# Strided attention scores and values in four quadrants of the array, and one engine for both query copies

## The chip, the core and the metric

The kernel runs on one core of one Trainium2 chip. The metric is the time of one execution on the device in microseconds, as the median of several runs; smaller is better. The core has a matrix engine (TensorE, PE in the profile, with its weight loads as PEld), a vector engine (VectorE, DVE), an activation engine (ScalarE, ACT), GpSimd (POOL) and SyncE (SP), which here issues DMA loads. TensorE writes its results to PSUM, eight banks of 2 KB in each of 128 partitions; the other engines read them from there.

## What is computed

Attention over 8 batches, 8 heads, 576 positions and 64 columns a head, and behind it a mixture of 8 experts. Four heads attend to the last 32 positions (local), the other four to the earlier positions with the same residue modulo 32 (strided). In short, from the reference:

```python
rel = pos[:, None] - pos[None, :]
mask_local = (rel >= 0) & (rel < 32)
mask_strided = (rel >= 0) & (pos[None, :] % 32 == pos[:, None] % 32)
scores = np.where(mask, q @ k.T / sqrt(64), -1e9)
attn = exp(scores - max); attn = attn / (sum(attn) + 1e-9)
x = attn @ v                      # (8*576, 512) for the experts
e = argmax(x @ w_gate + modality_bias)
out = gate * (relu(x @ w1[e]) @ w2[e])
```

So a strided head falls apart into 32 problems (residues) of 18 x 18 positions each.

## The kernel before, in words

Attention runs over 32 units, 16 local and 16 strided in turn (lines 965 to 972). A local unit is one head of two batches, a strided unit two heads of one batch. A step of the main loop (lines 1032 to 1076) works on four units at once: the scores of unit n, the transposes of unit n-2 (turn), the masks of unit n+1 and the value products of unit n-3; it also issues loads for units n+3 and n-1. Two steps, one strided and one local, are called a pair here, and a pair has the number of its strided unit, 0 to 15. After each 8 units a batch pair is complete: its rows are transposed (xl, xs), the router's products run (lg) and small steps on VectorE follow. Behind attention come the slots of the experts (L921, L935), which are not touched.

TensorE's order is the order of the code (manual_schedule, line 1029), and a few steps are pinned. The other engines' order, and which PSUM bank a tile gets, are chosen by a scheduler before the program runs. On the chip each engine works through its own list in order, and an instruction that waits holds up what stands behind it.

A strided unit before: prep copies the queries of the two heads into a tile qz whose other blocks are zero, one head by VectorE, one by ScalarE (L408). masks writes the mask into the score tile ss by a product with the identity (L412). scores makes 32 products (L419), one a residue: 36 stationary columns (two heads of 18 queries, 128 partitions high because qz has zeros) and 18 moving columns. VectorE takes the maximum (L431) and the difference (L433), ScalarE the exponential (L434), VectorE the row sum (L436), plus 1e-9 (L437), the reciprocal (L438) and the product (L440, tile ens). turn transposes in four pieces (tile ts) and spreads them into a block diagonal tile eb: VectorE writes two of four blocks (L450), ScalarE the others (L454). values makes 32 records from 16 products (L464) of 72 stationary rows, and ScalarE copies them from ot to xc (L472).

A local unit before: prep copies the queries of two batches into qd, one by VectorE and one by ScalarE (L317). Scores (L334) are followed by maximum and difference on VectorE for a tile of 256 and one of 320 columns (L341, L342), by exponentials on ScalarE (L343, L344), by transposes, by copies into et (L356, L359), by the products with the values (L369, L375) and by VectorE's normalisation (L380, L381, L382, tile xt). xl is copied by L495, xs by L488.

A float32 product shows as two matmul records and two weight loads in the profile.

Of the kernel before, what the change touches and what calls it, by code (L numbers as in the profile page):

```python
# [54 lines left out]
C_T = C_P + 1  # L55
C_F = C_T + 4
# [12 lines left out]
M_TRI = M_S + 16 * 18  # L69
# [13 lines left out]

def _constants():
# [7 lines left out]
    for t in range(4):  # L92
        cf[18 * t:18 * t + 18, C_T + t] = 1
# [13 lines left out]
    causal = np.where(a[None, :] <= a[:, None], 0, BIG)  # L107
    for j in range(2):
        for h in range(2):
            r0 = 64 * j + 18 * h  # L110
            cb[r0:r0 + 18, M_S:M_S + 288] = np.tile(causal, (1, 16))
# [6 lines left out]
def _layout(q, k, v, moe_modality_id, moe_w_gate, moe_modality_bias, moe_w1, moe_w2):  # L118
# [29 lines left out]
    vs = v[:, 4:].reshape(B, 2, 2, 18, 4, 2, 4, D).transpose(0, 1, 6, 3, 4, 5, 2, 7)  # L148
    vs = np.ascontiguousarray(vs).reshape(B, 2, 72, 1024)
# [33 lines left out]
def attention_moe(ctx: ExitStack, tc: tile.TileContext, a, out):  # L183
# [103 lines left out]
    qzs = zeros(2, [P, 32, 2, 18], "qz")  # L287
    for t in qds + ets:
        nc.vector.memset(t[:], 0.0)
    for t in qzs:  # L290
        nc.gpsimd.memset(t[:], 0.0)


    class Local:
# [92 lines left out]
    class Strided:  # L387
# [10 lines left out]
        def load_values(self, part, last):  # L398
            if part == 0:
                self.vs = lp.tile([72, 8, 2, D], F32, tag="vs", name=f"vs{self.n}")  # L400
                behind(nc.sync.dma_start(self.vs.rearrange("p g h d -> p (g h d)"), a["vs"][self.b, self.pr]), last)

        def prep(self):
            self.qz = qz = qzs[self.n % 2]
            for h in range(2):
                r = slice(64 * h, 64 * h + 64)
                dst, src = qz[r, :, h, :], self.qk[r, 0, :].rearrange("p (r q) -> p r q", q=18)
                pin(nc.scalar.copy(dst, src) if h else nc.vector.tensor_copy(dst, src))  # L408

        def masks(self):  # L410
            self.s = pa(f"ss{self.n}")[:, :288]
            nc.tensor.matmul(self.s, identb, cb[:, M_S:M_S + 288], start=True, stop=True)  # L412

        def scores(self):
            n, qz, s = self.n, self.qz, self.s
            for i in range(16):
                for j in range(2):
                    r = (i // 4) * 8 + j * 4 + i % 4
                    at["scores"] = nc.tensor.matmul(  # L419
                        s[64 * j:64 * j + 36, 18 * i:18 * i + 18],  # L420
                        qz[:, r, :, :].rearrange("p h q -> p (h q)"),
                        self.qk[:, 1, 18 * r:18 * r + 18],
                        start=False, stop=True, skip_group_check=True,
                    )
            s3 = s.rearrange("p (i k) -> p i k", i=16)

            def bc(t):
                return t.unsqueeze(2).to_broadcast([P, 16, 18])

            mx = lp.tile([P, 16], F32, tag="mxs", name=f"mxs{n}")  # L430
            nc.vector.tensor_reduce(mx[:], s3, AX.X, ALU.max)  # L431
            ex = lp.tile([P, 16, 18], F32, tag="exs", name=f"exs{n}")
            nc.vector.tensor_tensor(ex[:], s3, bc(mx), ALU.subtract)  # L433
            nc.scalar.activation(ex[:], ex[:], AF.Exp, scale=0.125)  # L434
            sm = lp.tile([P, 16], F32, tag="sms", name=f"sms{n}")
# [3 lines left out]
            self.en = lp.tile([P, 16, 18], F32, tag="ens", name=f"ens{n}")  # L439
            nc.vector.tensor_tensor(self.en[:], ex[:], bc(sm), ALU.mult)  # L440

        def turn(self):
            n = self.n
            tp = pa(f"ts{n}").rearrange("p (g q) -> p g q", g=4)
            for g in range(4):
                turned_to(tp[0:72, g, :], self.en[:, 4 * g:4 * g + 4, :])
            self.eb = eb = lp.tile([72, 8, 4, 36], F32, tag="eb", name=f"eb{n}")
            src = tp[0:72].rearrange("p g (j x) -> p (g j) x", j=2)[:, :, 0:36]
            sh = [72, 8, 2, 36]
            nc.vector.tensor_tensor(  # L450
                eb[:, :, 0:2, :], src.unsqueeze(2).to_broadcast(sh),
                cf[0:72, C_T:C_T + 2].unsqueeze(1).unsqueeze(3).to_broadcast(sh), ALU.mult)
            for t in (2, 3):
                nc.scalar.activation(eb[:, :, t, :], src, AF.Copy, scale=cf[0:72, C_T + t:C_T + t + 1])  # L454

        def values(self):
            n, eb, vs, b = self.n, self.eb, self.vs, self.b
            for g2 in range(2):
                ot = pa(f"ot{n}{g2}")[:, :288]
                for g in (2 * g2, 2 * g2 + 1):  # L460
                    for j in range(2):
                        c = (g % 2) * 144 + 72 * j
                        for h in range(2):
                            at["values"] = nc.tensor.matmul(  # L464
                                ot[64 * h:64 * h + 64, c:c + 72],
                                vs[:, 2 * g + j, h, :],
                                eb[:, 2 * g + j, :, 18 * h:18 * h + 18],
                                start=True, stop=True, skip_group_check=True,
                            )
                base = (b % 2) * S  # L470
# [676 lines left out]
```

## Time and profile before

| | before |
|---|---|
| median of 3 runs | 598.16 us (596.69 to 599.0) |
| profiled execution | 600.58 us |
| its span, first to last instruction | 598.8 us |
| TensorE busy | 574.2 us (96%) |
| VectorE busy | 439.1 us (73%) |
| ScalarE busy | 395.0 us (66%) |
| GpSimd busy | 249.0 us (42%) |
| mean granted TensorE clock | 0.986 |

A busy share is a mean over the span. Attention fills the first 163 us or so, and there the engines stand otherwise than in the rest; the stretches below are taken from it. "Idle before" names what ended a wait, not what caused it.

### The profile page before, as it was taken

Reading aid. Unit: us, or ns where it says so; the run is one execution under the profiler, and the core shown is the slowest. Engines: PE = TensorE matmul, PEld = TensorE weight load, DVE = VectorE, ACT = ScalarE, POOL = GpSimd, SP = SyncE. Lnnn points to the kernel's source line nnn. Section 1 sums busy time; section 2 is a strip of 40 time slices with the busy share of each in tenths; the row PEclk is TensorE's granted clock in tenths of the full one; section 3 lists DMA queues with packets and bytes.
Section 4 is the critical chain, followed back from the end, with each engine's and each line's share of the span. In section 5 each row is a group of like instructions: output and inputs, shape, how many; then the busy total and the mean of one; then the engine's idle time right before and its main releaser. Section 6 shows DMA issues by size and latency. Waiting matters only on the chain.

```text
span 598.8 us, 15262 instructions
## 1 busy us (share of the span) xinstructions
PE 574.2 (96%) x5995; PEld 508.0 (85%) x5997; DVE 439.1 (73%) x1092; ACT 395.0 (66%) x814; POOL 249.0 (42%) x226
## 2 busy tenths in 40 slices
PE   8998889897999999999999999999999999999995
PEld 5887778776879898999999989999999999999995
DVE  6885967954868799668687687687687787787542
ACT  5897868764785676676566576665665665665652
POOL 1021101126247636554544746546545646532311
PEclk9999989988899999999999999999999999999998
DMA  8997978987745843744843844213214239514631
GB/s 316 301 295 218 346 242 282 318 293 248 253 108 159 235 146 97 235 156 103 243 153 98 221 168 92 71 37 106 71 36 106 71 113 278 110 45 71 221 103 50
DMA packets 72482, 102.03 MB, mean 170 GB/s; under 512 B 48019, under 2 KB 48275, under 8 KB 68820
## 3 DMA queue, kind: packets, MB, share of 16 engines
q0 software_dynamic: 20672, 58.01, 29.1%
q1 hardware_dynamic: 51252, 42.48, 26.7%
q8 instruction: 49, 0.80, 0.6%
q10 hardware_dynamic: 480, 0.51, 0.3%
q14 instruction: 29, 0.24, 0.1%
HBM read 123.45 MB, written 19.18 MB: 238 GB/s over the span
## 4 chain that ended last, share of the span: by engine, by line
PE 85%; DVE 4%; issue 4%; DMA 3%; ACT 2%; POOL 0%; SPq 0%; POOLq 0%; ACTq 0%; DVEq 0%
PE h L921 34%; PE o L935 33%; PE o L369 3%; PE ot L464 2%; DMA vs<-in_vs 2%; PE s L334 2%; PE ss L419 2%; PE xs L218 1%; PE lg L524 1%; PE t L218 1%; PE ts L218 1%; PE xl L218 1%; DMA qks<-in_qks 1%; PE en L620 1%; ACT wh L956 1%
## 5 line engine op out<-in xcount | busy, mean ns | idle before, releaser
L957 DVE TENSOR_TENSOR wl<-raw,wh 128x512 fp32r<-128x512 f32 x288 | 187.8, 692 | 66.0 <-ACT wh L956 52.5
L956 ACT CAST wh<-raw 128x512 fp32r<-128x512 f32 x288 | 163.9, 619 | 71.5 <-PE o L935 49.5
L921 PE MATMUL h<-xh,wl 128*128 128x256 f32 x576 | 162.7, 283 | 0.0
L921 PE MATMUL h<-xl,wh 128*128 128x256 f32 x576 | 162.6, 283 | 0.0
L921 PE MATMUL h<-xh,wh 128*128 128x256 f32 x576 | 162.4, 282 | 0.2 <-ACT wh L956 0.2
L803 POOL DMA_INDIRECT raw<-in_w,wi x72 | 92.6, 1286 | 158.1 <-DVE wl L957 121.4
L921 PEld LDWEIGHTS h<-xh,wh 128*128 128x128 f32 x576 | 109.5, 190 | 7.6 <-issue 0.6
L921 PEld LDWEIGHTS h<-xl,wh 128*128 128x128 f32 x576 | 109.6, 190 | 5.5
L935 PE MATMUL o<-wh,hh 128*128 128x512 f32 x288 | 114.3, 397 | 0.0
L935 PE MATMUL o<-wl,hh 128*128 128x512 f32 x288 | 113.8, 395 | 0.0
L921 PEld LDWEIGHTS h<-xh,wl 128*128 128x128 f32 x576 | 109.7, 190 | 1.0
L935 PE MATMUL o<-wh,hl 128*128 128x512 f32 x288 | 110.3, 390 | 0.0
L924 ACT ACTIVATE hh<-h 128x256 fp32r<-128x256 f32 x144 | 55.4, 384 | 67.2 <-PE h L921 50.1
L926 DVE SCALAR_TENSOR_TENSOR hl<-h,hh 128x256 fp32r<-128x256 f32 x144 | 60.7, 421 | 30.7 <-ACT hh L924 23.4
L935 PEld LDWEIGHTS o<-wh,hl 128*128 128x128 f32 x288 | 53.5, 188 | 11.0
L935 PEld LDWEIGHTS o<-wh,hh 128*128 128x128 f32 x288 | 54.6, 189 | 7.8 <-ACT hh L924 0.2
L935 PEld LDWEIGHTS o<-wl,hh 128*128 128x128 f32 x288 | 54.6, 190 | 5.6
L943 POOL DMA_INDIRECT out<-y,le x36 | 44.2, 1229 | 20.7 <-ACT y L942 11.0
L794 POOL DMA_INDIRECT le<-ld,li x36 | 39.6, 1101 | 12.9 <-issue 10.1
L787 POOL DMA_INDIRECT fx<-xd,le x36 | 40.1, 1115 | 11.0 <-issue 10.7
L479 POOL DMA_DIRECT2D xd<-xt x20 | 14.5, 725 | 61.9 <-ACT xt L488 61.9
L369 PEld LDWEIGHTS o<-vv,et 128*64 128x64 f32 x512 | 21.2, 156 | 10.1 <-issue 7.6
(192 smaller groups left out, 779.8 us busy)
## 6 DMA issues: line engine op xcount, KB each, us to landing
vv<-in_vl SPq DMA_DIRECT2D x32, 292.5 KB
qks<-in_qks SPq DMA_DIRECT2D x32, 288.0 KB
xd<-xt POOLq DMA_DIRECT2D x16, 512.0 KB
qk<-in_qkl SPq DMA_DIRECT2D x16, 304.0 KB
qk<-in_qkl SPq DMA_DIRECT2D x16, 288.0 KB
vs<-in_vs SPq DMA_DIRECT2D x16, 288.0 KB
raw<-in_w,wi POOLq DMA_INDIRECT x72
xd<-xt POOLq DMA_DIRECT2D x4, 256.0 KB
```

The source lines that it names most:

```text
L218: at["turn"] = nc.tensor.transpose(dst, src, ident)
L369: at["values"] = nc.tensor.matmul(o[64 * jj:64 * jj + 64, k, :], et[:, u, :, :].rearrange("p g q -> p (g q)"), vv[:, u, :], start=True, st ...
L787: pin(nc.gpsimd.indirect_dma_start(xt[:, h, :], None, xd[0:xrows, :], IOA(ap=le[:, h, 0:1], axis=0)))
L794: pin(nc.gpsimd.indirect_dma_start(le[:, h, :], None, ld[0:xrows, :], IOA(ap=li[:, s, h:h + 1], axis=0)))
L803: pin(nc.gpsimd.indirect_dma_start(raws[j].rearrange("p f c -> p (f c)"), None, a["w"], IOA(ap=wi[:, s, j:j + 1], axis=0), bounds_check=E ...
L921: nc.tensor.matmul(hp, w[:, a1], x[:, c, :], start=(k == 0), stop=(k == 11))
L924: nc.scalar.activation(hh[:], hp, AF.Relu)
L926: nc.vector.scalar_tensor_tensor(hl[:], hp, 0.0, hh.bitcast(F32), ALU.max, ALU.subtract)
L935: nc.tensor.matmul(os[h], hx[:, m], w[:, 512:1024], start=(f == 0 and i == 0), stop=(f == 7 and i == 2))
L943: outs.add(pin(nc.gpsimd.indirect_dma_start(out, IOA(ap=le[:, h, 0:1], axis=0), y[:], None, bounds_check=NT - 1, oob_is_err=False)))
L956: nc.scalar.copy(wh[:, c], raw[:, c])
L957: nc.vector.tensor_tensor(wl[:, c], raw[:, c], wh[:, c].bitcast(F32), ALU.subtract)
```

## The change

Strided scores no longer use a zero-padded tile: qz and its two copies (L408) are gone. A product takes one head and three (or two) residues: 54 or 36 stationary columns, 54 or 36 moving columns, 64 partitions high. The two heads stand in the two halves of the partitions, and two groups of residues (j) in the two halves of the output columns, so that four products in a row use the four 64 x 64 quadrants. The products of different residues inside a 54 x 54 block are masked away by a new mask (three diagonal blocks of 18 x 18). The scores of a unit fill two PSUM tiles of 324 columns, one a head, instead of one of 288; 24 products instead of 32.

VectorE makes maximum and difference once for each tile; exponential, row sum and final product run over 12 x 54 = 648 columns instead of 288. The result en goes to one of two fixed tiles with zeroed padding. turn makes six transposes of 128 x 128 into two PSUM tiles instead of four, and ScalarE copies them plainly into eb (L461); the block diagonal is already there, so L450 and L454 and the constants C_T are gone. values makes 24 products instead of 16, 54 or 36 rows high, in the four quadrants (half of the residues by head). The values come in four DMAs (two of 54 x 512, two of 36 x 256 elements) instead of one of 72 x 1024. Of the local units one line changes: both copies of the queries are ScalarE's (L326). A pair takes 12 PSUM tiles instead of 10.

The changed lines in the file of after have numbers of their own: ss L422 (mask) and L432, mxs L444, exs L445 and L446, sms L448 to L450, en L452, eb L461, ot L473, xc L481, qd L326, mx L350, ex L351 on VectorE and L352, L353 on ScalarE, xt L391.

```diff
-    qzs = zeros(2, [P, 32, 2, 18], "qz")
+    ens = zeros(2, [P, 12, 64], "en")
...
-                pin(nc.scalar.copy(dst, src) if bb else nc.vector.tensor_copy(dst, src))
+                pin(nc.scalar.copy(dst, src))
...
+            c, rn = ((slice(0, 512), 54), (slice(512, 768), 36))[part]
+            dst = self.vs.rearrange("p a j h d -> p (a j h d)")
+            for half in range(2):
+                r = slice(64 * half, 64 * half + rn)
+                behind(nc.sync.dma_start(dst[r, c], a["vs"][self.b, self.pr, half, 0:rn, c]), last)
...
+            for sl in range(6):
+                for j in range(2):
+                    r0, nr = _residues(sl % 2, sl // 2, j)
+                    w, c = 18 * nr, slice(18 * r0, 18 * r0 + 18 * nr)
+                    for h in range(2):
+                        r = slice(64 * h, 64 * h + 64)
+                        at["scores"] = nc.tensor.matmul(
+                            self.s[h][64 * j:64 * j + w, 54 * sl:54 * sl + w], qk[r, 0, c], qk[r, 1, c],
+                            start=False, stop=True, skip_group_check=True,
+                        )
...
+            for i0, i1 in ((0, 4), (4, 6)):
+                tp = pa(f"ts{n}{i0}").rearrange("p (g q) -> p g q", g=4)
+                for i in range(i0, i1):
+                    turned_to(tp[:, i - i0, :], self.en[:, 2 * i:2 * i + 2, :])
+                nc.scalar.copy(eb[:, i0:i1, :], tp[:, 0:i1 - i0, :])
...
+            for ga in range(3):
+                for j in range(2):
+                    for half in range(2):
...
+                        for h in range(2):
+                            at["values"] = nc.tensor.matmul(
+                                ot[half][64 * h:64 * h + 64, c:c + w], vs[r, ga, j, h, :],
+                                eb[r, 3 * h + ga, 64 * j:64 * j + w],
```

Where the scheduler put things now, at three places. The first is ScalarE from a local unit's last small exponential (ex) to the strided exponential (exs) of the next strided unit, between units 2 and 3, before:

```order
L344 ACTIVATE ex_557<-ex_557 128x128
L472 COPY xc_120<-ot_609 128x16x18
L317 COPY qd_102<-qk_462 64x18x32
L454 ACTIVATE eb_683<-ts_678,cf_sb 72x8x36 x2
L408 COPY qz_105<-qks_554 64x32x18
L434 ACTIVATE exs_668<-exs_668 128x288
```

The same place of ScalarE's list after, between units 2 and 3:

```order
L353 ACTIVATE ex_552<-ex_552 128x128
L481 COPY xc_120<-ot_597 128x16x18
L481 COPY xc_120<-ot_598 128x16x18
L326 COPY qd_102<-qk_464 64x18x32 x2
L461 COPY eb_679<-ts_680 128x512
L461 COPY eb_679<-ts_686 128x256
L446 ACTIVATE exs_667<-exs_667 128x648
```

Both copies of ot now stand behind the last local exponential (before, one stood ahead of it), and both copies of the queries stand there too, while qz is gone.

The second place is VectorE from the strided row sum (sms) to the last local difference (ex) in the pair of unit 2, before:

```order
L436 TENSOR_REDUCE sms_501<-exs_498 128x16
L342 TENSOR_TENSOR ex_557<-s_519,mx_556 128x256
L341 TENSOR_REDUCE mx_556<-s_521 128x5
L437 TENSOR_SCALAR sms_501<-sms_501 128x16
L342 TENSOR_TENSOR ex_557<-s_521,mx_556 128x320
```

The same of VectorE after, in the pair of unit 2:

```order
L448 TENSOR_REDUCE sms_497<-exs_491 128x12
L390 RECIPROCAL rs_544<-rs_544 128x4
L350 TENSOR_REDUCE mx_551<-s_516 128x4
L449 TENSOR_SCALAR sms_497<-sms_497 128x12
L391 TENSOR_TENSOR xt_116<-o_535,rs_544 128x4x64
L350 TENSOR_REDUCE mx_551<-s_518 128x5
L351 TENSOR_TENSOR ex_552<-s_516,mx_551 128x256
L450 RECIPROCAL sms_497<-sms_497 128x12
L351 TENSOR_TENSOR ex_552<-s_518,mx_551 128x320
```

The first local maximum and the second product for xt, which stood ahead of the row sum, now stand behind it.

The third place is VectorE around the row sum in the pair of unit 3; before, its list there reads as in unit 2:

```order
L433 TENSOR_TENSOR exs_498<-ss_438,mxs_496 128x288
L380 TENSOR_SCALAR rs_534<-o_523 128x5
L381 RECIPROCAL rs_534<-rs_534 128x5
L382 TENSOR_TENSOR xt_116<-o_523,rs_534 128x5x64
L380 TENSOR_SCALAR rs_547<-o_538 128x4
L381 RECIPROCAL rs_547<-rs_547 128x4
L341 TENSOR_REDUCE mx_556<-s_519 128x4
L382 TENSOR_TENSOR xt_116<-o_538,rs_547 128x4x64
L408 COPY qz_106<-qks_395 64x32x18
L436 TENSOR_REDUCE sms_501<-exs_498 128x16
```

After, in the pair of unit 3:

```order
L445 TENSOR_TENSOR exs_667<-ss_594,mxs_666 128x324
L448 TENSOR_REDUCE sms_673<-exs_667 128x12
L389 TENSOR_SCALAR rs_707<-o_696 128x5
L449 TENSOR_SCALAR sms_673<-sms_673 128x12
L390 RECIPROCAL rs_707<-rs_707 128x5
L450 RECIPROCAL sms_673<-sms_673 128x12
L391 TENSOR_TENSOR xt_116<-o_696,rs_707 128x5x64
L389 TENSOR_SCALAR rs_720<-o_711 128x4
L452 TENSOR_TENSOR en_106<-exs_667,sms_673 128x12x54
L390 RECIPROCAL rs_720<-rs_720 128x4
L350 TENSOR_REDUCE mx_727<-s_692 128x4
L350 TENSOR_REDUCE mx_727<-s_694 128x5
```

The row sum stands directly behind the strided difference here, and all of the local output's normalisation and the strided final product (en) stand between it and the local maxima; the second product for xt and the two local differences follow. The pair of unit 4 has the same steps in between.

## Rows read from the trace of the kernel before

**Rows 1.** Busy time by stretch, in us; the first line names the columns.

```profile
core 0: us, PE busy (x) PEld busy (x) DVE busy (x) ACT busy (x) POOL busy (x), PEclk, DMA share, GB/s
15.63:28.90 13.27, 12.34 (x362) 11.12 (x360) 12.27 (x39) 11.45 (x27) 0.00 (x0) 1.00 0.99 312
28.90:36.27 7.37, 6.25 (x183) 5.59 (x181) 6.81 (x19) 6.97 (x16) 2.93 (x6) 1.00 1.01 290
36.27:44.42 8.15, 7.88 (x195) 7.03 (x193) 6.06 (x19) 7.04 (x16) 0.07 (x1) 1.00 0.97 292
44.42:58.37 13.95, 12.04 (x248) 9.80 (x246) 7.83 (x26) 10.32 (x24) 1.72 (x2) 1.00 0.68 199
58.37:65.80 7.43, 6.46 (x184) 5.72 (x182) 7.40 (x34) 7.19 (x18) 0.72 (x1) 1.00 1.01 379
65.80:73.15 7.35, 7.23 (x200) 6.62 (x198) 7.04 (x27) 6.19 (x15) 2.62 (x4) 1.00 1.04 319
73.15:85.27 12.12, 9.70 (x196) 8.74 (x194) 6.44 (x20) 6.75 (x17) 0.00 (x0) 0.86 0.81 262
```

**Rows 2.** TensorE in order of time, 48.7 to 63.3: start, length, line, tile.

```profile
48.83 1.93 PE L524 MATMUL lg<-xc,rt_sb 128*32 128x256 f32 x32
...
56.67 1.30 PE L419 MATMUL ss<-qks,qz 128*36 128x18 f32 x64
57.90 0.63 PE L218 MATMUL ts<-cf_sb,ens 128*72 128x128 f32 x4
...
61.78 1.22 PE L464 MATMUL ot<-eb,vs 72*64 72x72 f32 x32
```

**Rows 3.** ScalarE in order of time, 21.5 to 25.4.

```profile
21.51 0.42 ACT L343 ACTIVATE ex<-ex 128x256 f32<-128x256 f32 x1
21.82 0.30 ACT L344 ACTIVATE ex<-ex 128x128 f32<-128x128 f32 x1
22.02 0.64 ACT L472 COPY xc<-ot 128x288 f32<-128x288 f32 x1
22.68 0.67 ACT L317 COPY qd<-qk 64x576 f32<-64x576 f32 x1
23.38 0.88 ACT L454 ACTIVATE eb<-ts,cf_sb 72x288 f32<-72x288 f32 x2
24.29 0.67 ACT L408 COPY qz<-qks 64x576 f32<-64x576 f32 x1
24.98 0.44 ACT L434 ACTIVATE exs<-exs 128x288 f32<-128x288 f32 x1
```

**Rows 4.** VectorE in order of time, 24.6 to 28.3.

```profile
24.60 0.39 DVE L341 TENSOR_REDUCE mx<-s 128x4 f32<-128x256 f32 x1
24.91 0.42 DVE L382 TENSOR_TENSOR xt<-o,rs 128x256 f32<-128x256 f32 x1
25.24 0.45 DVE L408 COPY qz<-qks 64x576 f32<-64x576 f32 x1
25.60 0.44 DVE L436 TENSOR_REDUCE sms<-exs 128x16 f32<-128x288 f32 x1
25.96 0.41 DVE L342 TENSOR_TENSOR ex<-s,mx 128x256 f32<-128x256 f32 x1
26.30 0.48 DVE L341 TENSOR_REDUCE mx<-s 128x5 f32<-128x320 f32 x1
26.69 0.16 DVE L437 TENSOR_SCALAR sms<-sms 128x16 f32<-128x16 f32 x1
26.81 0.49 DVE L342 TENSOR_TENSOR ex<-s,mx 128x320 f32<-128x320 f32 x1
...
27.85 0.46 DVE L440 TENSOR_TENSOR ens<-exs,sms 128x288 f32<-128x288 f32 x1
```

**Rows 5.** Groups by line and shape, ScalarE, 5 to 165: busy, mean ns, idle.

```profile
L495 ACT COPY xc<-xl 128x512 f32<-128x512 f32 x12 | 6.8, 591 | 1.0 <-PE xl L218 0.9
```

**Rows 6.** Waits of VectorE, 5 to 165: us in total, times, longest.

```profile
DVE sms L436 <- ACT exs L434: 0.9, 2, 0.6
```

More of the change, by code (lines that the diff above doesn't have):

```diff
@@ L81, in _block, with _residues @@
     return (i + 2 * bb) % 18
+def _residues(half, a, j):
+    return (16 * half + 6 * a + 3 * j, 3) if a < 2 else (16 * half + 12 + 2 * j, 2)
 def _constants():
@@ L91, in _constants @@
     cf[:, C_F:C_F + 4] = P * np.arange(4)
-    for t in range(4):
-        cf[18 * t:18 * t + 18, C_T + t] = 1
     cb = np.zeros((P, M_N), np.float32)
@@ L107, in _constants @@
     causal = np.where(a[None, :] <= a[:, None], 0, BIG)
+    three = np.full((54, 54), BIG, np.float32)
+    for t in range(3):
+        three[18 * t:18 * t + 18, 18 * t:18 * t + 18] = causal
     for j in range(2):
-        for h in range(2):
-            r0 = 64 * j + 18 * h
-            cb[r0:r0 + 18, M_S:M_S + 288] = np.tile(causal, (1, 16))
+        cb[64 * j:64 * j + 54, M_S:M_S + 324] = np.tile(three, (1, 6))
     cb[:, M_TRI:M_TRI + P] = -(np.arange(P)[:, None] >= np.arange(P)[None, :]).astype(np.float32)
@@ L410, in masks @@
[L410 to L433, printed above, removed]
+                self.vs = lp.tile([P, 3, 2, 2, D], F32, tag="vs", name=f"vs{self.n}")
@@ new lines, in load_values, with masks @@
+            c, rn = ((slice(0, 512), 54), (slice(512, 768), 36))[part]
[3 more added lines that the diff above has]
+                behind(nc.sync.dma_start(dst[r, c], a["vs"][self.b, self.pr, half, 0:rn, c]), last)
+        def prep(self):
+            pass
+        def masks(self):
+            self.s = [pa(f"ss{self.n}{h}")[:, :324] for h in range(2)]
+            for s in self.s:
+                nc.tensor.matmul(s, identb, cb[:, M_S:M_S + 324], start=True, stop=True)
@@ L438, in scores @@
             nc.vector.reciprocal(sm[:], sm[:])
[L439 to L440 removed]
+            self.en = ens[n % 2]
+            nc.vector.tensor_tensor(self.en[:, :, 0:54], ex[:], bc(sm, 12), ALU.mult)
         def turn(self):
             n = self.n
[L444 to L446 removed]
@@ L447, in turn @@
[L447 to L454, printed above, removed]
+            self.eb = eb = lp.tile([P, 6, P], F32, tag="eb", name=f"eb{n}")
@@ L456, in values @@
+            for i0, i1 in ((0, 4), (4, 6)):
[3 more added lines that the diff above has]
+                nc.scalar.copy(eb[:, i0:i1, :], tp[:, 0:i1 - i0, :])
         def values(self):
             n, eb, vs, b = self.n, self.eb, self.vs, self.b
[L458 to L462, printed above, removed]
+            ot = [pa(f"ot{n}{half}")[:, :288] for half in range(2)]
@@ L463, in values @@
+            for ga in range(3):
+                for j in range(2):
+                    for half in range(2):
+                        r0, nr = _residues(half, ga, j)
+                        w, c = 18 * nr, 18 * (r0 - 16 * half)
+                        r = slice(64 * half, 64 * half + w)
                         for h in range(2):
                             at["values"] = nc.tensor.matmul(
-                                ot[64 * h:64 * h + 64, c:c + 72],
-                                vs[:, 2 * g + j, h, :],
@@ L472, in values @@
-                nc.scalar.copy(dst, ot.rearrange("p (r q) -> p r q", r=16))
+                dst = self.xc[:, base:base + S].rearrange("p (q r) -> p r q", r=32)[:, 16 * half:16 * half + 16, :]
+                nc.scalar.copy(dst, ot[half].rearrange("p (r q) -> p r q", q=18))
     rows = []
```

36 lines of the change are left out of this document (20 added, 16 removed).

## The prediction, made before the changed kernel was run

> **What bounds the kernel now.** I read the busy time by stretch first, cut at one place of the program, the masks of a local score tile, so that a stretch is one pair of units (one strided unit, one local unit) [rows 1]. The change touches only the attention stage, which ends near 163 us; what follows is the expert stage, and it starts when attention lets go of TensorE, so what attention gains or loses is gained or lost by the whole. The reader is to see in [rows 1] that no single engine bounds the pairs. In the two plain pairs from 15.63 to 28.90 a pair takes 6.64 us, TensorE is busy 6.17 of it, VectorE 6.14, ScalarE 5.73, and the DMA share is 0.99. From 58.37 to 65.80 VectorE is full (7.40 of 7.43) and ScalarE nearly (7.19). From 44.42 to 58.37, where one pair also carries the transposes and the router's products of a batch pair, TensorE is the long one (12.04 of 13.95). From 73.15 to 85.27 TensorE stands still for over 2 us (9.70 busy of 12.12) and then runs part of the stretch at 1.2 GHz instead of 2.4 (granted clock 0.86 on average).
>
> Then ScalarE and VectorE in order of time [rows 3, 4]. Both work through their lists without a gap. ScalarE goes from the second exponential of a local unit (21.51) to the end of the strided exponential (24.98 + 0.44 = 25.42) in 3.91 us. VectorE goes from the strided row sum L436 (25.60) to the end of the second local difference L342 (27.30) in 1.70 us. These two pieces close a ring: the row sum waits for the strided exponential, the second local exponential waits for the second difference, and each engine keeps its order. The ring is 3.91 + 1.70 and about 0.1 for two handovers, 5.7 us, and the pair takes 6.64: the ring has 0.9 us to spare. That fits the waits: VectorE waited for that exponential twice in the stage, 0.9 us in all [rows 6].
>
> **The change, part by part.** TensorE. A strided unit's scores take 1.23 us (64 records, 56.67 to 57.90) and its value products about 1.15 (32 records) [rows 2]. Their records run two at a time: 0.038 us per two of 36 stationary and 18 moving columns, 0.072 per two of 64 and 72. I take 0.055 for the new ones of 54 columns. There are now 48 records in each. Four at a time this is 12 rounds, 0.66 us each, 1.06 less in sum; two at a time it is 24 rounds, 1.32 each, 0.26 more in sum. Which holds, no row shows for quadrants: before, all products use the whole height of the array. The nearest row is the router's product, four strips of 32 columns [rows 2]: 32 records of 256 columns in 1.93 us, 0.060 each. At the value products' pace, 0.072 per two of 72 columns, 256 columns two at a time would be 0.128 each, so there four strips do run together. I take four. Two more transposes per unit (0.63 for four now, so 0.3) and a second mask product (0.2) are added. TensorE's sum is -0.5 us a pair, at worst +0.8. The Trainium skill, TensorEngine Tiling (Array Packing), section Theoretical Speedup, gives up to 2x for each small dimension, which for both products at once would be half of their 2.38 us; the sum above has that as its better end.
>
> VectorE. Away go L408 (0.36 from start to start [rows 4]), L317 (0.45, a copy of the same size) and L450 (576 elements, about 0.7 at 0.08 per 64 columns, as from 256 to 320 in L341 and L342). The five strided steps grow: the maximum and the difference run twice on 324 columns (0.40 each, as L341 on 320), the sum and the final product run on 648 elements instead of 288 (360 more, some 0.4: the sum L436 from 0.36 to 0.76, the product L440 from 0.46 to 0.86). All together +0.1 us a pair: nothing.
>
> ScalarE. Away go L408 (0.69 from start to start) and L454 (0.91 for two) [rows 3]; added are a second copy of the local queries (0.70), two plain copies out of PSUM (0.59 by L495 [rows 5], and 0.34 for half the width by the slope of L343 to L344) and 360 more elements in the strided exponential (0.44 becomes 0.80). That is +0.4 us a pair on an engine that is busy 5.7 to 7.2.
>
> Queues. The strided values come in four DMAs instead of one, the same bytes. SP issues three more per pair; the pieces land two units ahead of their use, behind the same waits on TensorE as the loads around them. I cost this at nothing; it is hidden by the lead, and in stretches with a DMA share of 1.0 it could cost some tenths a pair in the first four pairs, 1 us in all at most.
>
> The ring. This is where the sum is decided, and it comes from the two orders shown above. On ScalarE both copies of ot (L481) and both copies of the queries (L326) now stand between the last local exponential and the strided one; before, one L472 and one L317 did. From the second local exponential to the end of the strided one: exponential, small exponential and first copy of ot 1.17 (21.51 to 22.68 [rows 3]); second copy 0.6; queries 0.70 twice; eb 0.55 and 0.35; exponential 0.80. Sum 4.9 instead of 3.9. On VectorE the row sum now stands ahead of both maxima of the local scores and the normalisation of the second local output: sum 0.76, maximum 0.31, product 0.4, maximum 0.39, difference 0.34, difference 0.49 and three small ones, 0.4 together by L437's 0.12 from start to start [rows 4], 3.1 us instead of 1.7. The ring is 4.9 + 3.1 + 0.1 = 8.1 us, over the 6.64 of the pair. It now decides: ScalarE waits for the differences, VectorE for the exponential, each with work of its own that is queued behind the wait. In the pairs of strided units 3 and 4 the order is longer still: the final product (0.86) and the other normalisation (0.49, as L342 on 320 columns, and three small ones, 0.4) stand in between as well, 4.8 us, and the ring is 9.8.
>
> **The sum**, by pairs of [rows 1], named by strided unit. Units 1 and 2: 2 x 8.1 - 13.27 = +2.9. Unit 3: 9.8 - 7.37 = +2.4. Unit 4: 9.8, and four more copies by ScalarE (L504, before L495, three of 0.59 and a small one: 1.9) between the queries and eb: 11.7 - 8.15 = +3.5. Unit 5: TensorE's transposes and products stand between, so the ring is slack; TensorE gains some tenths, ScalarE's 0.4 takes them: 0. Unit 6: 8.1 and 0.3 for the router's small steps among them: +1.0. Unit 7: its order is short (row sum, maximum, two differences): ring 7.1, under 7.35: 0. Unit 8: 8.1 and 1.9 for the four copies, 10.0 against 12.12, of which over 2 us are TensorE's standstill; about half of that still shows: -1.1. Units 5 to 8 add nothing. Units 9 to 12 repeat the pattern: 0. The last three pairs hold stalls that a pair with slack on TensorE hides in part: -1. Total 2.9 + 2.4 + 3.5 + 0 + 0 - 1 = +7.8; unit 1 may still run by the first loads rather than by the ring, so I take +7.5. The profiled execution took 600.58 us for a span of 598.80, and stands 2.4 over the median of 598.16. The difference is made on it and put on the median: 605.7, rounded to 605.5.
>
> Bounds of the term: with the shorter spacings (products that overlap the next by 0.2 us) the ring is 7.3, and the first four pairs cost 5 instead of 8.8; with the value of whole durations it is 8.6 and they cost 11. So the ring by itself gives 601.5 to 609.
>
> **The rivals.** First, the ring slips: the engines are ahead of it and ScalarE is just full. A plain pair is then ScalarE's 7.0 us (5.73 busy and the small gaps between, plus 0.4, bounded by the pair's 6.64 + 0.4): units 1 and 2 cost +0.7, the rest nothing, TensorE gains 0.5 in units 5, 8, 9 and 12, and the total is -1 to +2: 598.5. For it speaks that ScalarE has 0.1 to 1 us idle per pair now; against it that the order on each engine is fixed. The Trainium skill, TensorEngine Tiling (Array Packing), section PSUM Bottleneck, speaks against the change in this way: after a TensorE speedup the copies out of PSUM may become the limit. By it the time would be this rival's; [rows 1] leave room for it, with ScalarE at 5.7 to 7.2 us of a pair before the change.
>
> Second, faster: the pairs follow TensorE. It is the longest in units 5, 8, 9 and 12 and close in 4 and 7; if ring and ScalarE stay hidden there, 0.5 us in each of 16 pairs is the ceiling, 8 us, and half of it likely, for VectorE and DMA are full in the rest: 594. The Trainium skill, TensorEngine Tiling (Array Packing), section Theoretical Speedup, points to this side.
>
> Third, the quadrants don't do what they are meant to: the two heights of the array run one after the other. TensorE then takes 0.8 more per pair; under an 8.1 us ring it is hidden in the plain pairs and shows in the ones where TensorE is long, and with waits between its short bursts TensorE may fall to 1.2 GHz, as after the standstill in [rows 1], each fall some 1.7 us ((1 - 0.86) x 12.12): 610 to 616.
>
> The side that the forecast's sign turns on is the ring: below 6.6 us the plain pairs lose nothing and the second rival decides; above it each tenth costs 0.1 us a pair.
>
> **How the numbers follow.** Ring decides (605.5): 0.63. ScalarE just full (598.5): 0.16. Faster (594): 0.13. Quadrants one after the other (613): 0.08. Half a per cent, 3 us, is about what a measurement of this kernel can tell from no change. Of the ring's 0.63 some 0.05 lies within 3 us. So: faster 0.14, same 0.20, slower 0.66. The range takes in the ring's 601.5 to 609, most of the second case and half of the last: 597 to 613.
>
> **What the changed profile would show.** VectorE waiting at the row sum L448 for the strided exponential, over 1 us in plain pairs and about 3 in units 3 and 4, where before it was 0.9 in the whole stage. ScalarE waiting at L352 for the differences. Plain pairs of 8 to 10 us. TensorE's scores at 0.6 to 0.7 us (0.66 shows four at a time, 1.3 two), with idle time before the strided transposes. The expert stage unchanged in length. Wrong would be plain pairs still at 6.6 us, or a row sum that does not wait.

## The result and the profile after

| | before | after |
|---|---|---|
| median | 599.0 us | 605.04 us |
| ratio to before | | 1.0144 (95%: 1.0109 to 1.0178) |
| the same, measured again on another chip | 598.28 us | 604.59 us, 1.0104 (1.0071 to 1.0138) |
| profiled execution, its span | 600.58, 598.8 us | 607.44, 605.6 us |

The changed kernel is slower by 6 us in the median; 605.5 was forecast, in 597 to 613. The ratios leave out executions that were clearly slower than the others of the same kernel, so they need not equal the quotient of the medians. The expert stage did not move: from its first product to the end of the span it takes 435.2 us before and 435.7 after. All of the loss lies in attention, whose last strided exponential ends at 154.65 before and at 160.54 after.

Busy time by stretch, cut at the same masks, after; the first row answers to the first of [rows 1] (13.27 us there), the next four to its next four:

```profile
core 0: us, PE busy (x) PEld busy (x) DVE busy (x) ACT busy (x) POOL busy (x), PEclk, DMA share, GB/s
16.07:30.43 14.36, 12.17 (x369) 10.54 (x366) 12.19 (x38) 11.93 (x28) 0.00 (x0) 1.00 0.92 291
30.43:40.26 9.83, 6.71 (x185) 5.76 (x183) 6.66 (x19) 6.86 (x16) 2.65 (x6) 0.95 0.73 237
40.26:50.98 10.72, 8.93 (x198) 7.59 (x197) 6.01 (x19) 8.20 (x18) 0.00 (x0) 0.89 0.69 207
50.98:62.96 11.98, 11.66 (x250) 9.13 (x249) 6.91 (x23) 9.38 (x22) 1.73 (x2) 1.00 0.69 226
62.96:71.79 8.83, 6.47 (x187) 5.43 (x185) 7.89 (x33) 7.27 (x19) 0.72 (x1) 1.00 0.95 336
```

In 30.43 to 40.26 no engine is busy for more than 6.86 of 9.83 us, and the DMA share has fallen to 0.73, where [rows 1] had 1.01: everything waits for something. What it waits for stands in the order of time. First VectorE, then ScalarE, in the pairs of units 2 and 3:

```profile
26.02 0.83 DVE L448 TENSOR_REDUCE sms<-exs 128x12 f32<-128x648 f32 x1 [1.30 <-ACT exs L446]
...
28.43 0.43 DVE L351 TENSOR_TENSOR ex<-s,mx 128x320 f32<-128x320 f32 x1
...
33.54 0.83 DVE L448 TENSOR_REDUCE sms<-exs 128x12 f32<-128x648 f32 x1 [2.33 <-ACT exs L446]
...
37.52 0.80 DVE L351 TENSOR_TENSOR ex<-s,mx 128x256 f32<-128x256 f32 x2
...
42.99 0.83 DVE L448 TENSOR_REDUCE sms<-exs 128x12 f32<-128x648 f32 x1 [2.14 <-ACT exs L446]
```

```profile
25.25 0.74 ACT L446 ACTIVATE exs<-exs 128x648 f32<-128x648 f32 x1
...
28.42 0.90 ACT L352 ACTIVATE ex<-ex 128x256 f32<-128x256 f32 x2 [0.43 <-DVE ex L351]
29.22 0.29 ACT L353 ACTIVATE ex<-ex 128x128 f32<-128x128 f32 x1
29.54 1.16 ACT L481 COPY xc<-ot 128x288 f32<-128x288 f32 x2
30.49 1.36 ACT L326 COPY qd<-qk 64x576 f32<-64x576 f32 x2
31.88 0.86 ACT L461 COPY eb<-ts 128x512 f32<-128x512 f32 x2
32.76 0.74 ACT L446 ACTIVATE exs<-exs 128x648 f32<-128x648 f32 x1
...
37.96 0.81 ACT L352 ACTIVATE ex<-ex 128x256 f32<-128x256 f32 x2 [0.93 <-DVE ex L351]
...
42.22 0.74 ACT L446 ACTIVATE exs<-exs 128x648 f32<-128x648 f32 x1
```

This is the ring. The row sum starts at 26.02, when the exponential of unit 2 has ended (25.99); the second local difference ends at 28.86; its exponential, the second of the two at 28.42, starts at 28.90; ScalarE works through without a gap to the end of the next strided exponential, 33.50; the next row sum starts at 33.54. That is 2.91 us and 4.60 us, 7.51 in all. In unit 3 it is 33.50 to 38.36 to 42.96: 4.86 and 4.60, 9.46 in all. These are the pieces of [rows 3] and [rows 4], which took 3.91 and 1.70 before. The waits of the stage, VectorE's and ScalarE's (compare [rows 6]):

```profile
DVE sms L448 <- ACT exs L446: 5.8, 3, 2.3
...
ACT ex L352 <- DVE ex L351: 8.5, 11, 1.7
```

For what follows, the **period of unit k** is the time from the end of its strided exponential to the end of the next, read from the rows of that line, units counted from 0. A stretch of the stage is hard to compare between executions: in two executions of the kernel after, units 1 to 4 took 35.5 and 36.5 us and units 6, 7 and 10 25.3 both times, but the remaining eight periods 88.0 and 83.6. The first two groups serve as a ruler, good to about a microsecond; the ratios give the whole.

| kernel | units 1, 2, 3, 4 | sum | units 6, 7, 10 | sum | ratio to before (95%) |
|---|---|---|---|---|---|
| before | 6.8, 6.6, 7.2, 8.6 | 29.2 | 7.1, 7.3, 7.1 | 21.6 | 1 |
| after | 7.9, 7.5, 9.5, 10.7 | 35.5 | 9.0, 7.3, 9.0 | 25.3 | 1.0144 |
| after, second trace | 7.9, 7.5, 9.1, 12.0 | 36.5 | 9.0, 7.3, 9.0 | 25.3 | 1.0104 |
| copies_alone | 7.2, 6.9, 6.9, 8.7 | 29.6 | 6.7, 7.1, 6.9 | 20.7 | 1.000 (0.996 to 1.004) |
| quads_alone | 7.9, 7.0, 9.0, 11.1 | 35.0 | 9.1, 7.5, 8.8 | 25.4 | 1.011 (1.003 to 1.020) |
| sum_late | 8.3, 7.2, 7.5, 10.7 | 33.7 | 7.8, 7.8, 8.0 | 23.6 | 1.011 (1.006 to 1.016) |
| turn_late | 7.7, 6.9, 9.0, 8.7 | 32.3 | 8.0, 7.8, 8.9 | 24.6 | 1.011 (1.007 to 1.014) |
| late_both | 7.0, 7.9, 7.7, 9.8 | 32.3 | 8.0, 7.3, 8.1 | 23.4 | 1.000 (0.997 to 1.004) |
| sum_twice | 8.7, 9.7, 9.7, 10.2 | 38.2 | 9.3, 11.1, 8.7 | 29.1 | 1.026 (1.022 to 1.030) |
| before_late | 8.0, 6.4, 9.9, 8.6 | 32.8 | 7.7, 7.7, 7.7 | 23.0 | 1.007 (1.004 to 1.010) |

### The profile page after: what moved, and what is told of

The parts are those of the page before. It is cut to its first block, busy times and chain, and to the rows that moved or that the text cites. A ratio compares the mean times of both kernels' runs of the same rounds, so it can differ in the third digit from the quotient of the medians.

```text
span 605.6 us, 15386 instructions
## 1 busy us (share of the span) xinstructions
PE 569.7 (94%) x6045; PEld 500.7 (83%) x6045; DVE 441.5 (73%) x1076; ACT 399.6 (66%) x814; POOL 235.8 (39%) x226
## 4 chain that ended last, share of the span: by engine, by line
PE 73%; DVE 9%; ACT 9%; issue 6%; POOL 1%; DMA 1%; POOLq 0%; ACTq 0%
PE h L930 32%; PE o L944 31%; ACT qd L326 2%; PE o L378 2%; ACT xc L481 2%; PE s L343 2%; PE lg L533 1%; DVE sms L448 1%; DVE mx L350 1%; DVE ex L351 1%; ACT et L365 1%; PE xs L227 1%; DVE xt L391 1%; ACT wh L965 1%; DVE en L452 1%
## 5 line engine op out<-in xcount | busy, mean ns | idle before, releaser
L812 POOL DMA_INDIRECT raw<-in_w,wi x72 | 82.9, 1152 | 173.5 <-DVE wl L966 131.6
L803 POOL DMA_INDIRECT le<-ld,li x36 | 39.3, 1093 | 12.8 <-issue 10.4
```

Of the source, the lines that this page charges most:

```text
L803: pin(nc.gpsimd.indirect_dma_start(le[:, h, :], None, ld[0:xrows, :], IOA(ap=li[:, s, h:h + 1], axis=0)))
L812: pin(nc.gpsimd.indirect_dma_start(raws[j].rearrange("p f c -> p (f c)"), None, a["w"], IOA(ap=wi[:, s, j:j + 1], axis=0), bounds_check=E ...
```

## The experiments

**The two parts of the change, each alone.** Both copies of the local queries on ScalarE, in the kernel before:

```diff
-                pin(nc.scalar.copy(dst, src) if bb else nc.vector.tensor_copy(dst, src))
+                pin(nc.scalar.copy(dst, src))
```

> The kernel before with one part of the change: both copies of the local queries on ScalarE, the strided heads as they were. The order on the engines is otherwise that of before. Theory (the ring decides): ScalarE's piece of the ring grows by 0.70 us, the ring from 5.7 to 6.4, still under the 6.64 of a plain pair; only the pairs with four more copies (units 4 and 8) come near it. So 0 to +1.5 us against the kernel before. Rival (each copy costs its time on a full ScalarE): 0.7 us in some eight pairs, +5 us or more.

Measured: 603.93 us against 603.74, ratio 1.000. The ring theory's number: 16 copies of 0.67 us more on ScalarE cost nothing that the interval (0.4% to either side) shows. It fits that the ring before had room for one; VectorE's waits at the row sum rose from 0.9 to 2.2 us in the stage. And the quadrants with the copies as they were (the line the other way round, in the kernel after):

```diff
-                pin(nc.scalar.copy(dst, src))
+                pin(nc.scalar.copy(dst, src) if bb else nc.vector.tensor_copy(dst, src))
```

> The kernel after with that part undone: one of the two copies of the local queries back on VectorE, where it stands behind the last local difference and so outside the ring. Theory (the ring decides): the ring is 0.70 shorter, 7.4 in units 1 and 2 and 9.0 in 3 and 4, so each ring-bound pair (eight or nine of sixteen) gets 0.5 to 0.7 back: -4 to -6 us against the kernel after, which leaves 0 to +2 against the kernel before. Rival (quadrants themselves cost it, by their transposes, banks or transfers): no more than 1 us comes back, +5 against the kernel before.

Measured: ratio 1.011 (1.003 to 1.020), units 1 to 4 at 35.0 instead of 35.5. The expectation fails: half a microsecond of the expected 4 to 6 came back. Units 2 and 3 gave 0.5 us each, as expected, but unit 1 gave nothing and unit 4 was 0.5 longer. ScalarE's piece did get shorter, and the row sum of unit 2 waited 0.48 us instead of 1.30, but something else was then late. TensorE, around that row sum:

```profile
27.71 0.76 PE L432 MATMUL ss<-qks 64*54 64x54 f32 x46
29.37 0.85 PE L227 MATMUL ts<-cf_sb,en 128*128 128x128 f32 x6 [0.91 <-DVE en L452]
```

TensorE stands at the strided transposes for the shares (en), and behind them in its list stand the next local scores, which VectorE needs for its next differences. The copy went back to VectorE ahead of en (28.05 to 28.49, en from 28.41), so it delayed the shares by 0.36 us, about half of the 0.67 that it took out of ScalarE's piece. I read this as a second ring: shares, transposes, local products and scores, local difference, row sum, shares.

**The first ring opened.** The row sum and what follows it are written behind the next local unit's scores and pinned there; nothing else is touched:

```diff
             nc.scalar.activation(ex[:], ex[:], AF.Exp, scale=0.125)
+            self.exs = ex
+        def shares(self):
...
-            nc.vector.tensor_reduce(sm[:], ex[:], AX.X, ALU.add)
+            pin(nc.vector.tensor_reduce(sm[:], ex[:], AX.X, ALU.add))
...
             units[n].scores()
+        if n % 2 == 0 and 2 <= n <= nu:
+            units[n - 1].shares()
```

> The kernel after with one thing moved: VectorE's row sum of the strided shares (and with it the three steps behind it) stands behind the second local difference instead of ahead of it, in every pair. No work is added or taken away. Theory (the ring decides): the ring is open, ScalarE no longer waits for a VectorE that waits for ScalarE; a plain pair is then the busy time of ScalarE or VectorE, about 7.0 us instead of 7.5 to 9.5: -4 to -7 us against the kernel after, so -1 to +2 against the kernel before. Rival (PSUM banks, 12 tiles a pair from 8 banks, hold TensorE): the bank of the second output tile comes free somewhat earlier, so -2 at most. Rival (the quadrants' own work): 0.

Measured: 1.011 (1.006 to 1.016), no gain that shows in the whole. The wait at the row sum is gone from the trace, unit 3 falls from 9.5 to 7.5, units 6 and 10 by 1.2 and 1.0; but now TensorE stands at the transposes in seven of the sixteen units (0 to 3, 6, 10 and 14), as here:

```profile
28.18 0.74 PE L432 MATMUL ss<-qks 64*54 64x54 f32 x48
30.40 0.84 PE L227 MATMUL ts<-cf_sb,en 128*128 128x128 f32 x6 [1.49 <-DVE en L460]
```

My expectation of 4 to 7 us left this out: a later row sum makes the shares later, and the transposes were already waiting 0.55 us for them in this place in the kernel after. That this wait sets the pair is not shown, though. VectorE's list is nearly full here: between these two steps, 7.2 us apart, the trace shows no other wait of VectorE.

```profile
25.08 0.17 DVE L389 TENSOR_SCALAR rs<-o 128x5 f32<-128x5 f32 x1 [0.41 <-PE o L384]
...
32.27 0.16 DVE L389 TENSOR_SCALAR rs<-o 128x5 f32<-128x5 f32 x1 [0.41 <-PE o L384]
```

So TensorE's wait may as well be for a VectorE that is the longest by itself. A second reason clouds the whole of this run and is told at the end: a stretch near 147 us in which TensorE crawled.

With one copy on GpSimd on top of it:

```diff
-                pin(nc.scalar.copy(dst, src))
+                pin(nc.scalar.copy(dst, src) if bb else nc.gpsimd.tensor_copy(dst, src))
```

> The kernel of the run before (row sum behind the local differences) with one of the two copies of the local queries on GpSimd instead of ScalarE. Theory: with the ring open the busy time of ScalarE and VectorE decides; ScalarE's falls from about 6.9 to 6.2 a pair, VectorE's stays at 6.9, so -0 to -2 us against the kernel with the row sum moved alone, and -0 to -3 against the kernel before. Rival: the copy on GpSimd holds VectorE up or comes late for the local scores: +1 or more against the run before.

Measured: 1.009 (1.005 to 1.013). Nothing that can be told from the run before it; its trace has the same waits at the transposes (4.3 us in 4 for en) and a new one, 4.0 us for a copy that stood on GpSimd behind the router's set-up.

**Both rings opened.** On top of sum_late, the strided transposes move on TensorE from behind the strided scores to behind the local value products:

```diff
-        if 2 <= n <= nu + 1:
+        if 2 <= n <= nu + 1 and n % 2 == 0:
             units[n - 2].turn()
...
             units[n - 3].values()
...
+        if 2 <= n <= nu + 1 and n % 2:
+            units[n - 2].turn()
```

> The kernel after, unchanged, beside the three of this set on the same chip: the measure for them, and a second trace that shows which of its stalls come back. Both theories: 1.010 to 1.018 times the kernel before; the waits at the row sum (2 us in units 3 and 4) and at the second output tile come back at the same places, waits of TensorE that no semaphore explains need not.

> The kernel after with two things moved: the row sum behind the second local difference, as in the earlier run, and the strided transposes on TensorE from behind the strided scores to behind the local value products, so that TensorE no longer stands 1.6 to 2.1 us at them for the late shares. No work is added or taken away. Theory (two rings of nearly the same length: exponential to row sum to difference to exponential, and shares to transposes to local scores to difference to shares; opening one only shows the other): with both open a plain pair is the 6.8 to 7.0 us of VectorE's or ScalarE's own work: 3 to 6 us less than the kernel after on the same chip. Rival (VectorE's and ScalarE's own work is what costs): no more than 1 us less. Rival (a third wait, on PSUM banks or the turned shares): no change or slower.

Measured on one chip: after 604.59 us, ratio 1.0104; late_both 597.53, ratio 1.0003 (0.9965 to 1.004). By the ratios six microseconds come back, all that the change had cost, with every product, copy, transfer and PSUM tile of the change in place. By the ruler it is half: these seven units take 60.8 us in after, 55.7 here and 50.8 before. The profiled execution of late_both took 603.09 us, 5.6 more than its median, so the trace shows where waits went, and the six microseconds stand on the ratios. VectorE's rows of late_both, by line and shape (busy us, mean ns, idle before), and its plain pairs:

```profile
L444 DVE TENSOR_REDUCE mxs<-ss 128x6 f32<-128x324 f32 x32 | 14.3, 487 | 2.7 <-PE ss L432 2.7
L460 DVE TENSOR_TENSOR en<-exs,sms 128x648 f32<-128x648 f32 x16 | 13.3, 834 | 0.5
L456 DVE TENSOR_REDUCE sms<-exs 128x12 f32<-128x648 f32 x16 | 13.1, 818 | 0.0
```

```profile
15.40:29.42 14.02, 12.17 (x375) 10.13 (x367) 13.31 (x37) 11.32 (x26) 0.00 (x0) 1.00 0.98 296
```

The row sum no longer waits (0.0), and VectorE is busy 13.31 of 14.02 us: with the order opened, these two plain pairs are close to VectorE's own work, about 6.7 us of 7.0. Over the stage it is not full; it waits 19.6 us in 10 times at the local maxima for TensorE (10.6 in 6 in after).

The fourth corner, the transposes moved and the row sum left where it was:

> The kernel after with one thing moved: the strided transposes on TensorE stand behind the local value products; the row sum stays ahead of the second local difference. It is the fourth corner beside the row sum moved alone, both moved, and none moved. The move also takes the two eb copies out of ScalarE's piece of the first ring (they come behind the strided exponential now), so that piece is 4.2 us instead of 4.9, VectorE's 2.7 to 3.1, the ring 7.0 to 7.4 instead of 8.1. Theory (two rings, sized by their rows): 2 to 5 us less than the kernel after, less than with both moved. Rival (the gain of both moved came from the transposes' place alone): all of the 6 us.

Measured: 1.0105 (1.0071 to 1.0139). By the ruler units 1 to 4 gain 3.2 us, inside the expected 2 to 5, most of it in unit 4, while unit 3 takes 9.0 (9.5 and 9.1 in the two traces of after); VectorE still waits at the row sum:

```profile
DVE sms L448 <- ACT exs L446: 3.6, 3, 1.3
```

In the whole nothing of it shows, and this trace too has the crawling stretch. So neither move alone is worth anything that the ratio shows, and both together are worth 6 us by it. The ruler does not say the same: against the first trace of after it gives 3.5 us for the row sum alone, 3.9 for the transposes alone and 5.1 for both. That it takes both moves is therefore not shown.

**More time inside the ring.** The row sum run twice:

```diff
             nc.vector.tensor_reduce(sm[:], ex[:], AX.X, ALU.add)
+            pin(nc.vector.tensor_reduce(sm[:], ex[:], AX.X, ALU.add))
```

> The kernel after with the strided row sum run twice (the second result is the first): 0.75 us more on VectorE per strided unit, inside the ring. VectorE has 45 us of idle time in the attention stage, so by its share of busy time the addition is free. Theory (the ring decides): 0.75 us in each ring-bound pair, some eight or nine of sixteen: +5 to +7 us against the kernel after. Rival (no ring; TensorE, banks or transfers decide): 0 to +2.

Measured: 614.70 us, ratio 1.0262 against 1.0104 of the kernel after on the same chip, so 1.58% of the time before: +9.5 us. VectorE was idle for 45 us of the stage and had no room for 12 us more. In unit 1, where VectorE's list is otherwise nearly that of after, the period grows by 0.78 us, the length of the added step (0.74 from start to start). This is the one unit that shows it plainly. In units 2 and 7 the added step also changed the list (the shares moved ahead of the local differences there), and they grow by 2.1 and 3.8, part of why it is more than the 5 to 7 us expected. Units 3 and 4, where the ring was longest, change by +0.2 and -0.4: in unit 4 the shares moved behind the differences, and in unit 3 steps of the same list took some 0.5 us longer in the trace of after (the addition of 1e-9 took 0.54 us there, 0.16 here), for a reason that no run shows. The run rules out that a pair has room for the step; it does not show 0.75 us in each pair.

**Is it a gain of the moves themselves?** The same two moves in the kernel before:

> The kernel before with the same two moves (row sum behind the second local difference, strided transposes behind the local value products); the strided heads stay as they were. Theory (before, the ring had 0.9 us to spare, and pairs ran by the engines' own work): 0 to -2 us against the kernel before. Rival (the two moves are a gain of their own, whatever the strided heads do, and only hide a loss by the quadrants): -4 us or more, so that the quadrants would still cost 4 to 6 us beside it.

Measured: 605.90 us against 601.89, ratio 1.007 (1.004 to 1.010): slower, which neither side expected. The moves are no gain of their own. A wait that grows there is at another handover; ScalarE's largest wait, first in the kernel before, then with the moves:

```profile
ACT eb L454 <- DVE eb L450: 7.5, 8, 2.4
```

```profile
ACT eb L462 <- DVE eb L458: 15.3, 10, 4.3
```

Before, half of eb is made by VectorE, and with the transposes later it stands behind the local output's normalisation. The profiled execution of this kernel took 600.22 us, 5.7 less than its median, so its trace does not show the 0.7%, and that this wait costs it is not shown. Set side by side under the same order, before_late has a ratio of 1.007 and late_both of 1.000 (on two chips, with intervals that only just do not meet), and the ruler gives 55.8 and 55.7 us. So the order that gives the changed kernel its time back takes some from the kernel before.

**Can it beat both?** Three more steps on top of late_both, first one copy of the queries on GpSimd (the line of late_pool):

> The run before with one of the two copies of the local queries on GpSimd instead of ScalarE. Theory: with both rings open ScalarE's 0.6 us a pair less shows only where ScalarE is the longest: 0 to -2 us against the run before. If the rings are not what costs: 0.

Measured: 1.0001 (0.9972 to 1.0029), no change against the run before. Both sides allowed for that, so it decides nothing. Its trace has one wait for that copy:

```profile
PE s L343 <- POOL qd L326: 3.2, 1, 3.2
```

That unit's copy back on ScalarE:

```diff
-... if bb else nc.gpsimd.tensor_copy(dst, src))
+... if bb or self.n == 4 else nc.gpsimd.tensor_copy(dst, src))
```

> Both moved and one copy of the local queries on GpSimd, except for one unit, whose copy on GpSimd stood behind the router's set-up (TensorE waited 3.2 us for it in the trace); that one stays on ScalarE. Theory: 3 us less than the run with the copy on GpSimd everywhere, so -2 to -4 against the kernel before; plain pairs follow VectorE at 6.8 to 7.0. Rival: the wait was filled by slack and comes back elsewhere: 0.

Measured: 1.0005 (0.9973 to 1.0037), no gain. The wait went and another stands in its place, in the same pair (the rival's answer):

```profile
PE o L378 <- ACT qd L326: 2.2, 1, 2.2
```

And the shares on GpSimd:

```diff
-            nc.vector.tensor_tensor(self.en[:, :, 0:54], ex[:], bc(sm, 12), ALU.mult)
+            nc.gpsimd.tensor_tensor(self.en[:, :, 0:54], ex[:], bc(sm, 12), ALU.mult)
```

> The run before with the last of the strided steps of VectorE (the shares, exponentials times reciprocals, 0.80 us) on GpSimd. If VectorE's own work is what bounds the plain pairs once both rings are open, each plain pair gives some tenths up to 0.8: -2 to -6 us more. If GpSimd takes over 1.5 us for it, or stands behind its own transfers, TensorE waits at the transposes for it: slower than the run before.

Measured: 1.0053 (1.0021 to 1.0085), slower. Units 2 and 7 fall from 7.0 and 7.25 to 6.75 and 6.1, which fits that VectorE bound them, but units 6 and 10 rise from 7.8 and 8.25 to 9.4. GpSimd takes 1.27 us where VectorE took 0.83:

```profile
L460 POOL TENSOR_TENSOR en<-exs,sms 128x648 f32<-128x648 f32 x16 | 20.4, 1273 | 80.8 <-PE xs L227 31.2 <-DVE sms L458 23.6 <-DVE sml L590 10.5
```

The Trainium skill, GPSIMD Engine Reference, section Engine selection, has such two-input work at about half of VectorE's speed; here it is 1.27 to 0.83, so 1.5 times as long. What makes units 6 and 10 longer is not settled: GpSimd stays under the 1.5 us of the expectation, and TensorE waits nowhere at the transposes for the shares.

## Why the prediction was right, step by step

**TensorE.** Four at a time holds: the strided scores take 0.74 to 0.76 us as a length (0.66 forecast, 1.30 for 64 records in [rows 2]) and the value products 0.91 in late_both, where no wait stands among them (1.22).

```profile
28.03 0.91 PE L481 MATMUL ot<-eb,vs 54*64 54x54 f32 x48
28.75 0.74 PE L432 MATMUL ss<-qks 64*54 64x54 f32 x48
```

The Trainium skill, TensorEngine Tiling (Array Packing), section Theoretical Speedup, has up to 2x for each small dimension; scores gained 1.7 and values 1.3. TensorE's busy time in attention (up to the first expert product) fell from 146.0 to 141.5 us, 0.28 a pair, somewhat less than the 0.5 taken. The rival of quadrants in turn is out.

**VectorE and ScalarE.** VectorE's busy time in attention rose from 121.2 to 124.2 us, 0.2 a pair (0.1 taken); ScalarE's from 120.5 to 123.0, 0.15 a pair (0.4 taken). The value DMAs cost nothing that the waits show (TensorE waits 1.0 us for them, 0.9 before).

**The ring** was sized well in units 1 to 4. Taken 4.9 and 3.1 us for a plain pair, measured 4.60 and 2.91; taken 9.8 for unit 3, measured 9.46. Period by period, after less before: units 1 and 2 +2.0 (taken +2.9), unit 3 +2.2 (+2.4), unit 4 +2.1 (+3.5). The four together +6.3, and +7.3 in the second trace of after, for +8.8. The markers came too: 1.30, 2.33 and 2.14 us of waiting at the row sum of units 2, 3 and 4, somewhat less than written in units 3 and 4, and the same 5.8 us in three waits in the second trace. They came in these three pairs alone, and the plain pairs of units 1 and 2 took 7.9 and 7.5 us, not 8 to 10. The bounds were added up a little wide: from the prediction's own terms the ring gives 602.5 to 608, not 601.5 to 609.

**The rest of the sum** came out right by mistakes that cancel. Units 5 to 8: +0.9, taken -0.1. In it unit 6 is +1.9 (taken +1.0), and not by the ring: VectorE is full there, and no row sum waits. After, then before:

```profile
66.40:75.42 9.02, 7.87 (x212) 6.56 (x208) 8.85 (x38) 6.52 (x16) 1.49 (x2) 1.00 0.91 300
```

```profile
61.73:68.84 7.11, 6.14 (x181) 5.58 (x181) 6.98 (x32) 6.25 (x15) 0.00 (x0) 1.00 1.03 326
```

Before, the same period had 32 steps of VectorE, 6.98 busy of 7.11; the scheduler now puts six more into it. Unit 10 is the same, +1.9, and I had put 0 for units 9 to 12 after finding +1.0 in unit 6: the step failed by its own logic, since unit 10 repeats unit 6. Units 9 to 12 gave +2.8 in this trace (-0.6 in the second), the last ones -3.6 (taken -1), the start -0.5.

**What the prediction did not see.** First, the bank. The third of the strided value products, the first into the second output tile, waits for the PSUM tile that the local output's second normalisation frees, behind the row sum:

```profile
35.66 0.32 PE L473 MATMUL ot<-eb,vs 54*64 54x54 f32 x4
37.70 0.83 PE L473 MATMUL ot<-eb,vs 54*64 54x54 f32 x42 [1.72 <-issue]
```

```profile
PE ot L473 <- issue: 6.8, 7, 1.7
```

The trace calls it "issue"; but the normalisation (L391) had ended at 37.60, 0.1 earlier, and at 27.66 for 27.76 in the pair before, and late_both, where it is early, has no such wait. Five of the seven waits (5.2 us) end 0.1 us behind that normalisation; before, the waits of this name were 1.7 us in 4. The Trainium skill, TensorEngine Tiling (Array Packing), section Gotcha 1: PSUM Pressure, has different row tiles write to different PSUM banks; this kernel does so, and that it must no run here shows. In units 1 to 4 these waits cost no more on top of the ring: the strided differences were ready 1.9, 1.6, 1.4 and 1.3 us before ScalarE came to the exponential. And sum_late has 1.2 us of them left, turn_late 0.8, and neither gains in the ratio.

Second, and this is where the reasoning fell short though the number held: I wrote that the plain pairs lose nothing once the ring is below 6.6 us. With the order opened, units 1 and 2 together still take 15.5 us (sum_late) and 14.9 (late_both), against 15.4 in after and 13.4 before. VectorE is busy for 14.2 and 13.5 us of these, so there the ring had cost little beyond that engine's own work; the units that gain in both runs are 3, 6 and 10. I take the wait at the transposes for a second ring, of nearly the same length as the first; its length was not measured, and VectorE's full list would explain quads_alone and sum_late as well. What the runs show is that the first ring sets units 2 and 3, where both of its ends wait (the rows), and that the six microseconds of the ratio are the price of an order, not of the work (late_both). That both rings are the cause together is my reading.

## What to carry to other kernels

Where engines keep their order, look for the loops that run through two or three of them and add up each loop's pieces, not the busy time of an engine; a step added to the loop that decides costs its whole length, however idle the engine is on average (0.78 us for a step of 0.74 in unit 1 of sum_twice), as long as the lists stay as they are, and one added to a loop that still has room costs nothing that shows (copies_alone). When the longest loop is found, look for the next limit before moving anything, be it another loop or the full list of one engine: in quads_alone a copy of 0.67 us taken from ScalarE made VectorE's shares 0.36 us later. A change that makes TensorE shorter should be tried together with a new order of the steps it waits for: here the order was worth all that the change had cost by the ratio, and still no gain was left; in the plain pairs VectorE's own 6.7 us then stood in the way. And the kernel before should be given the same order: it became slower by it, so each kernel has to be compared in the order that suits it.

## What was not expected of the hardware

In some executions TensorE crawls in one stretch near the end of attention, where GpSimd issues the look-ups for the experts. In sum_late:

```profile
147.00:154.00 7.00, 4.02 (x48) 2.75 (x49) 1.65 (x8) 3.48 (x8) 5.78 (x8) 0.50 0.72 226
```

The granted clock there is 0.50, 1.2 GHz, and the strided scores come in bursts with pauses:

```profile
149.51 0.34 PE L432 MATMUL ss<-qks 64*36 64x36 f32 x3 [0.31 <-issue]
150.28 0.31 PE L432 MATMUL ss<-qks 64*36 64x36 f32 x2 [0.43 <-issue]
151.00 0.26 PE L432 MATMUL ss<-qks 64*36 64x36 f32 x1 [0.41 <-issue]
```

No semaphore stands behind the pauses. The pauses began before the clock fell: the value products stood 0.44 and 0.43 us ahead of 143.37 and 144.12, and the granted clock is 1.00 up to 144.2 us and 0.50 from 144.5 on. The period of that unit, 13, is 20.4 us here, 20.2 in turn_late, 19.7 in quads_alone, 20.0 in late_pool and 19.2 in late_best; it is 13.2 and 12.8 in the two traces of after, 12.7 in late_both and 15.7 in before. Seven microseconds are more than the whole effect of the change. Whether a kernel's timing brings this stretch about or it falls on some executions of any of them was not tried; it may also go with the chip, since all five of these traces come from two chips (12 and 0) and the four of a third (chip 9) have none (12.2 to 14.8). So it stays open how much of the missing gain of sum_late and turn_late it took. That it need not show in the ratio, late_best tells, with the stretch in its trace and 1.0005 on the chip where turn_late had 1.0105. The six microseconds rest on late_both and after on chip 9.
